# Block-summary attention and two feed-forward layers: the first batch's values loaded whole and summed from the window tiles, four groups scored without a key copy, and the start-up order written out

## The chip, the cores and the metric

One core of a Trainium2 chip runs the whole kernel. The metric is the device time of one execution in microseconds (us); of several runs the median counts. The engines are named as the profile names them: PE (TensorE), DVE (VectorE), ACT (ScalarE), POOL (GpSimd), and SP (SyncE), which here only issues DMAs.

## The reference

Attention with a local window and block summaries, then two feed-forward layers in a row. Cut to what matters:

```python
# q, k, v: (B=2, H=8, S=768, D=64); block 32, window 16; nb = 24 blocks
k_sum = k.reshape(B, H, nb, 32, D).max(axis=3)
v_sum = v.reshape(B, H, nb, 32, D).mean(axis=3)
scores_l = where(|i - j| < 16, q @ k.T / 8, -1e9)
scores_s = q @ k_sum.T / 8 + log(32)
a = softmax(concat([scores_l, scores_s]))
x = a @ concat([v, v_sum])                    # -> (1536 tokens, 512)
h = x @ w_in;  x = maximum(0.01 * h, h) @ w_out        # 512 -> 2048 -> 512
h = x @ w_in2; out = (h * tanh(softplus(h))) @ w_out2
```

All inputs are float32, and the weights are split in the kernel into a high and a low part, so that each product is three passes on PE.

## The kernel before

**Attention.** Tokens and heads are cut into 24 groups: group g is one batch, one chunk of 256 tokens and one pair of heads (four pairs for a chunk, so groups 0 to 3 are the first chunk of batch 0, 0 to 11 are batch 0). A group goes through these steps. The one-letter names are those that the change uses, and the prediction uses them for both kernels, though only the kernel after has them in its code.

- q, v: DMA of the group's queries (`load_q`, 128 KB) and of its window of values (`load_vw`, 192 KB, into rows 0 to 95 of a tile `vw`, whose rows 96 to 119 are to hold the block means).
- C, D: POOL lays the group's keys (C, two instructions) and block maxima (D) into a tile `kw` of 120 columns for each 64 queries (`k_window`, L261).
- S: PE computes the scores (L367), in 16 instructions for a group. M: DVE adds the mask and finds the maxima (L381). E: ACT takes the exponentials (L391). I: DVE inverts the sums (L400, L401). N: POOL multiplies (L406).
- T: PE transposes (L412). P: ACT or DVE copies the result out of PSUM (L420, L422). A: PE multiplies by `vw` (L431). X and L: high part (ACT L448 or DVE L450) and low part (DVE L446) of the result go into the tile x.
- K, k, J: block maxima of the keys (`k_sum`, DVE L298) for batch 0 (K) and 1 (J, with the DMAs k).
- s, p: the block means of the values of batch 0. Before, two DMAs of 768 KB bring all values of batch 0 once more (`load_v0`), PE sums them with a matrix of 1/32 (`sum_v0`, L317), and ACT or DVE copies the sums from PSUM into rows 96 to 119 of four `vw` tiles (`place_v0`, L327, L329). The four tiles serve all chunks; only their rows 0 to 95 are loaded anew for a new chunk, once A of the chunk before has read them. Batch 1 has its own way (r, R, Z: `load_vs`, `sum_vs`, `place_vs`).

**Feed-forward.** The weights come in blocks of 512 KB: w is the DMA, t (ACT L130) and m (DVE L137) build the float, h (ACT L166 or DVE L164) and l (POOL L173) split it. PE works through slots: U.2n and U.2n+1 are the two halves of slot n's product with `w_in` (L465), G and g the activation (ACT L476, L477, DVE L481), O.2n and O.2n+1 the halves of its product with `w_out` (L520), three slots later. Slots 0 to 2 take the first 256 tokens with the weight rows 0 to 2, slots 3 to 5 the next 256 tokens, slots 6 to 8 all 512 tokens with rows 3 to 5; U.12 is the first half-slot of 512 tokens.

**Order.** From the start to the end of attention (15 slots) the order of the steps is made by a planner in the kernel, `run_order` (L829): each step has a duration, an engine, needs, a due time and buffers to take, and the planner simulates the engines and writes the steps out. PE, ACT, DVE and POOL then run their instructions in exactly that order; an instruction that waits holds up all that stands behind it on its engine. The DMAs go out of SP in the order written, and at most eight are in flight (a DMA takes over the semaphore of the one eight places ahead of it and waits for its landing). In gaps that the planner sees on PE it puts `warm`, products of zeros that go nowhere. After slot 15 the rest of the kernel is written plainly, and is the same in both kernels.

Of the kernel before, what the change touches and what calls it, by code (L numbers as in the profile page):

```python
# [28 lines left out]
def kernel(  # L29
# [274 lines left out]
    def load_v0(i, eng):  # L304
        t = bigp.tile([P, 3, H * D], F32, tag=f"big{i}", name="v0")
        dma(eng, t, v0[i * 3 * P:(i + 1) * 3 * P, :].rearrange("(t p) f -> p t f", p=P))
        vraw[0, i] = t

    def sum_v0(i, tag):
        if i == 0:  # L310
            vs[0] = bank(tag)
        t = vraw.pop((0, i))

        for j in range(3):
            x = 4 * (3 * i + j)
# [109 lines left out]
    def av(g):  # L425

        px, t = st[g]
        w = vw[groups[g][2]]
        for n in range(NB):
            for s in range(2):  # L430
                nc.tensor.matmul(  # L431
                    px[s * D:(s + 1) * D, n * QB:(n + 1) * QB],
                    w[:, n, s, :],
                    t[:, s * (NB // 2) + n // 2, (n % 2) * QB:(n % 2 + 1) * QB],
                    start=True, stop=True,
                )
        st[g] = px
# [137 lines left out]
    if True:  # L575
# [48 lines left out]

        store = {
            "bank": ["a0", "a1", "y0", "y1", "y2", "y3"], "h": ["h", "h"], "raw": [0] * 3, "top": [0] * 2,
            "mid": [0] * 4, "q": [], "kw": [0] * 4, "s": [0] * 4, "pT": [0] * NPT, "g": [0] * (LAG + 1), "t": [0] * 2,
        }
        held = {}
        closed = [False]  # L630

        def load(fn, mb, needs=(), turn=0.0, take=(), give=()):
            return step({"SP": mb}, fn, needs, turn, take, give)

        def later(f, *a):
            return lambda eng: f(*a)

        def given(x, end):
            x.end = end
            return x  # L640


        landed = [4.1, 5.4, 7.7, 9.0]
        K = {(0, h): given(step({}, None), landed[h]) for h in range(4)}
        Q = {g: given(step({}, None), landed[g] + 0.2) for g in range(4)}
        W_LOAD, W_TOP, W_MERGE, W_HI, W_LO = {}, {}, {}, {}, {}

        def need_slot(i):
            return i if i < 2 * nA else 100

        for i in range(2 * nA):
            u = need_slot(i)
            W_LOAD[i] = load(later(w_load), 0.524, [], max(u - 7, -4.1) if i else -5, [("raw", ("raw", i))])
        for i in range(2 * nA, 2 * nA + 7):
            W_LOAD[i] = load(later(w_load), 0.524, [], 8 + i - 2 * nA, [("raw", ("raw", i))])
        V0 = [load(later(load_v0, i, SP), 0.786, [], -4.7 + i / 10) for i in range(2)]
        VW = {g: load(later(load_vw, g, SP), 0.196, [], -4.4) for g in range(4)}
        SUM0 = []
        for i in range(2):
            def f(eng, i=i):  # L660
                sum_v0(i, held["vs"])
            SUM0.append(step({"PE": (0.9, 0)}, f, [V0[i]] + SUM0, -4, [("bank", "vs")] if i == 0 else ()))
        PLACE = {}
        for h in range(4):
            def f(eng, h=h):
                place_v0(h, eng)
            PLACE[0, h] = step(
                {"act": (0.58, 0), "dve": (0.69, 0)}, f, [SUM0[1]], -4 + h / 10, (), ["vs"] if h == 3 else (), h
            )
# [368 lines left out]
```

## Time and profile before

| | |
|---|---|
| time, median of 3 runs | 607.79 us (606.29 to 608.97) |
| profiled execution | 608.53 us, of which its span is 606.4 us |
| PE busy | 596.3 us, 98% of the span, 3334 matmul instructions |
| DVE, ACT, POOL busy | 382.4, 314.1, 194.0 us |
| DMA | 52.10 MB, mean 86 GB/s |
| mean granted TensorE clock | 0.994 |

The profile is of one execution. PE is busy nearly all the time, so the page's table of costly groups says little about a change at the start; what is to be read there are the first 70 us, by stretches, by the order of time on PE, and by the landings of the DMAs. A granted clock of 1.00 is 2.4 GHz, 0.50 is 1.2 GHz.

### The profile page before, as it was taken

How to read it: one execution, taken by the hardware profiler on the slowest of the kernel's cores; microseconds unless marked ns; L12 is line 12 of the kernel's file. 1: busy time of each engine (PE TensorE's matmuls, PEld its weight loads, DVE VectorE, ACT ScalarE, POOL GpSimd, SP SyncE). 2: the span in 40 equal slices, each digit the busy share in tenths (PEclk: the TensorE clock that was granted, in tenths of full speed). 3: DMA queues.
4: the chain of work that ended last, by engine and by line, in shares of the span. 5: the costliest groups of instructions: out<-in, count | busy, mean ns of one | idle time of the engine just before them, and what ended most of it. 6: DMA issues, size and time to landing. Idle time of an engine off the chain costs nothing.

```text
span 606.4 us, 9153 instructions
## 1 busy us (share of the span) xinstructions
PE 596.3 (98%) x3334; PEld 485.9 (80%) x3334; DVE 382.4 (63%) x777; ACT 314.1 (52%) x671; POOL 194.0 (32%) x214
## 2 busy tenths in 40 slices
PE   9889999999989999999999999999999999999997
PEld 7789878787868888888888888888888888888885
DVE  6779777356541113112636898777699998778684
ACT  4868957447762223123665745444457555445442
POOL 6657643245430001001631233323322322332221
PEclk9979999999999999999999999999999999999999
DMA  9986554016851000002346310000021000001011
GB/s 325 358 270 211 168 191 124 2 36 217 264 178 36 0 2 0 1 0 70 123 135 234 99 35 1 0 1 0 1 70 71 0 1 1 1 34 37 0 71 69
DMA packets 19373, 52.10 MB, mean 86 GB/s; under 512 B 2176, under 2 KB 5248, under 8 KB 19072
## 3 DMA queue, kind: packets, MB, share of 16 engines
q1 hardware_dynamic: 18752, 51.00, 24.9%
q8 instruction: 26, 0.43, 0.3%
q10 hardware_dynamic: 576, 0.52, 0.3%
q14 instruction: 19, 0.16, 0.1%
HBM read 48.37 MB, written 3.15 MB: 85 GB/s over the span
## 4 chain that ended last, share of the span: by engine, by line
PE 89%; DMA 4%; ACT 3%; DVE 2%; POOL 1%; issue 1%; SPq 0%; DVEq 0%; ACTq 0%
PE h L465 40%; PE y L527 21%; PE y L520 19%; DMA raw<-in_moe_w_out_dram 3%; PE a L431 2%; PE a L367 2%; PE a L412 2%; ACT top L130 1%; DVE mid L137 1%; PE y L541 1%; PE h L220 1%; DMA kT<-in_kT_dram 1%; POOL w L173 1%; DMA raw<-in_moe_w_in_dram 1%; ACT g L477 0%
## 5 line engine op out<-in xcount | busy, mean ns | idle before, releaser
L465 PE MATMUL h<-x,w 128*128 128x512 f32 (+1 forms) x1188 | 289.7, 390 | 0.2 <-POOL w L173 0.2
L465 PEld LDWEIGHTS h<-x,w 128*128 128x128 f32 x1188 | 219.0, 189 | 49.7 <-ACT g L477 0.4
L520 PE MATMUL y<-g,w 128*128 128x512 f32 (+1 forms) x612 | 145.6, 384 | 2.1 <-ACT yp L557 1.7
L527 PE MATMUL y<-w,g 128*128 128x512 f32 x552 | 136.9, 394 | 0.0
L194 POOL TENSOR_TENSOR g<-e,g 128x512 fp32r<-128x512 f32 x47 | 73.9, 1572 | 186.9 <-ACT g L191 179.4
L520 PEld LDWEIGHTS y<-g,w 128*128 128x128 f32 x612 | 110.0, 188 | 26.8 <-ACT yp L557 2.2
L527 PEld LDWEIGHTS y<-w,g 128*128 128x128 f32 x552 | 103.8, 188 | 24.0
L173 POOL TENSOR_TENSOR w<-mid,w 128x512 fp32r<-128x512 f32 x45 | 62.9, 1405 | 122.2 <-ACT w L166 117.9
L481 DVE TENSOR_TENSOR g<-t,g 128x512 fp32r<-128x512 f32 (+1 forms) x51 | 34.5, 679 | 89.6 <-ACT g L477 89.6
L137 DVE SCALAR_TENSOR_TENSOR mid<-raw,top 128x512 int32<-128x512 int32 x64 | 55.3, 871 | 29.9 <-POOL w L173 23.7
L476 ACT ACTIVATE t<-h 128x512 f32<-128x512 f32 (+1 forms) x51 | 28.9, 567 | 83.5 <-PE h L465 83.5
L130 ACT ACTIVATE top<-raw 128x512 f16<-128x512 bf16 x64 | 50.6, 796 | 29.0 <-DMA raw<-in_moe_w_out_dram 12.6
L492 ACT ACTIVATE e<-h 128x512 f32<-128x512 f32 x48 | 28.6, 597 | 70.8 <-PE h L465 64.2
L503 DVE SCALAR_TENSOR_TENSOR u<-u,r 128x512 f32<-128x512 f32 x48 | 37.1, 773 | 25.4 <-ACT r L496 25.1
L495 ACT ACTIVATE r<-u,two 128x512 f32<-128x512 f32 x48 | 34.8, 724 | 30.7 <-DVE u L494 30.7
L391 ACT ACTIVATE s<-s,nm 128x120 f32<-128x120 f32 x96 | 36.5, 382 | 18.0 <-DVE nm L381 17.8
L166 ACT CAST w<-mid 128x512 fp32r<-128x512 f32 x62 | 37.8, 618 | 14.1 <-DVE mid L137 8.3
L191 ACT CAST g<-e 128x512 fp32r<-128x512 f32 x48 | 29.5, 615 | 18.1 <-DVE e L505 17.9
L494 DVE SCALAR_TENSOR_TENSOR u<-e 128x512 f32<-128x512 f32 x48 | 34.6, 721 | 1.1
L406 POOL TENSOR_TENSOR s<-s,r 128x480 f32<-128x480 f32 x24 | 24.7, 1033 | 31.9 <-DVE r L401 29.8
L504 DVE SCALAR_TENSOR_TENSOR u<-u,r 128x512 f32<-128x512 f32 x48 | 33.2, 691 | 1.4
L505 DVE SCALAR_TENSOR_TENSOR e<-e,u 128x512 f32<-128x512 f32 x48 | 33.1, 690 | 1.1
(71 smaller groups left out, 444.4 us busy)
## 6 DMA issues: line engine op xcount, KB each, us to landing
raw<-in_moe_w_in_dram SPq DMA_DIRECT2D x32, 512.0 KB, 4.0
raw<-in_moe_w_out_dram SPq DMA_DIRECT2D x32, 512.0 KB, 3.5
vw<-in_vW_dram SPq DMA_DIRECT2D x24, 192.0 KB, 4.3
kT<-in_kT_dram SPq DMA_DIRECT2D x8, 400.0 KB, 7.2
out_dram<-yp SPq DMA_DIRECT2D x12, 256.0 KB, 2.0
q<-in_qT_dram SPq DMA_DIRECT2D x20, 128.0 KB, 5.1
vS<-in_vS_dram SPq DMA_DIRECT2D x2, 1024.0 KB, 6.4
v<-in_v_dram SPq DMA_DIRECT2D x2, 768.0 KB, 7.8
```

Source lines behind the costliest of these rows:

```text
L130: nc.scalar.mul(out=do, in_=di, mul=4.0)
L137: nc.vector.scalar_tensor_tensor(out=d, in0=wraw.pop(i)[:, 0:2 * DM].rearrange("p (f w) -> p f w", w=2)[:, :, 1], scalar=13, in1=wtop.pop( ...
L166: nc.scalar.copy(out=w[:, 0], in_=wmid[i])
L173: (eng or nc.gpsimd).tensor_sub(out=w[:, 1], in0=wmid.pop(i), in1=w[:, 0].bitcast(F32))
L194: (nc.vector if lo == "dve" else nc.gpsimd).tensor_sub(out=dst_lo, in0=src, in1=dst_hi.bitcast(F32))
L391: nc.scalar.activation(out=s[:, n], in_=s[:, n], func=AF.Exp, scale=-1.0, bias=nm[:, n:n + 1], accum_out=sm[:, n:n + 1],)
L465: nc.tensor.matmul(ph[:, 0:n], w[:, a, kt * P:(kt + 1) * P], x[:, c, kt, o:o + n], start=(kt == 0 and i == 0), stop=(kt == KT - 1 and i == 2),
L494: V.scalar_tensor_tensor(out=u, in0=e, scalar=2.0, in1=e, op0=ALU.add, op1=ALU.mult)
L495: nc.scalar.activation(out=r, in_=u, func=AF.Ln, bias=two[:, 0:1])
L503: V.scalar_tensor_tensor(out=u, in0=u, scalar=2.0, in1=r, op0=ALU.add, op1=ALU.mult)
L520: mm = nc.tensor.matmul(y[d][:, o:o + n], w[:, a, d * P:(d + 1) * P], g[:, c, 0:n], start=sta and not second, stop=sto,)
L527: nc.tensor.matmul(y[d], g[:, a, d * P:(d + 1) * P], w[:, c], start=sta, stop=sto,)
```

## The change

- The planner goes. A string, ORDER, lists every step up to the end of attention; a suffix a, d or p names the engine where there is a choice, and the names behind a colon are the PSUM banks.
- All twelve `vw` tiles of batch 0 exist at once (groups 4 to 11 in the two tiles `big0`, `big1`), all are loaded at the outset, and `sum_v0` sums from them in three parts (s.0 to s.2). The DMAs `load_v0` go. The sums are copied into four tiles from PSUM as before (p.0 to p.3), and from these into the other eight (p.4 to p.11) by DVE or POOL.
- Groups 0 to 3 are scored straight from the loaded keys and from the maxima: no C and D, and two products where there was one (96 and 24 columns), so 32 instructions for a group.
- Groups 4 to 7 are scored and multiplied singly, not in pairs. Their queries, and the weight blocks 3 and 4, are loaded early into a tile `early`, in the place of a part of x that is needed later.
- `warm` multiplies 128x128 by 128x128, where it was 64x64 by 64x128; there are 4, 3, 2 and 1 of them in the order, behind the ten at the outset, which stay.
- Some steps change engine (t.0, t.8 and t.12 go from ACT to POOL).

```diff
+    ORDER = """
+        q.6 K.0 C.4 q.5 q.4 K.1 C.5 S.0:a0,a1 q.7 D.5 S.1:y0,y1 D.4 v.2 M.0 C.6 E.0 w.0 K.2 v.1 C.7 v.3 warm.4
+        S.2:a0,a1 I.0 v.0 K.3 N.0 v.5 v.6 M.1 D.6 v.11 warm.3 T.0:y2 E.1 D.7 v.4 M.2 S.3:y0,y1 P.0d v.7 E.2
+        S.4:a0,a1 t.0p I.1 v.8 M.3 v.10 C.8 M.4 E.3 v.9 D.8 warm.2 s.0:y0 N.1 w.1 I.2 w.2 m.0 E.4 T.1:a0 w.3 I.3 N.2
+        S.5:a1,y1 q.9 P.1d q.8 h.0a N.3 M.5 T.2:y3 w.4 E.5 s.1 P.2d l.0 w.5 I.4 k.0 T.3:a1 s.2 I.5 N.4 P.3a k.2 N.5
+        T.4:y1 p.1a p.0d p.2a p.5d p.8p p.3a p.9d warm.1 A.2 p.6d q.11 t.1a C.9 p.4d A.0 p.11d t.2a X.2d p.7p A.1
+        L.2 X.0a T.5:y0 v.12 p.10p P.4d X.1a A.3 k.1 P.5a L.1 q.10 D.9 L.0 S.6:a0,y3 X.3a L.3 U.0 C.10 M.6 k.3 E.6
+        S.7:a1,y2 D.10 m.1 A.5 M.7 C.11 w.6 h.1a A.4 I.6 D.11 X.5a S.8:a0,a1 t.3a N.6 L.5 v.14 J.0 X.4a E.7 C.12
+        T.6:y0 q.13 L.4 U.1 l.1 J.2 q.12 v.15 G.0 I.7 m.2 U.2 P.6a v.13 m.3 t.4a U.3 w.7 J.1 N.7 h.2a A.6 t.5a M.8
+        l.2 T.7:y1 X.6a G.1 P.7d h.3a D.12 U.4 M.9 C.13 E.8 A.7 D.13 L.6 l.3 J.3 S.10:a0,a1 r.0 E.9 I.8 g.0 g.1 q.14
+        U.5 M.10 N.8 q.15 X.7a U.6 L.7 G.2 C.14 I.9 U.7 E.10 M.11 C.15 O.0 N.9 U.8 E.11 I.10 D.15 U.9 D.14 N.10
+        T.8:a0 G.3 I.11 T.9:a1 m.4 P.8a O.1 P.9a R.0 N.11 U.10 h.4a t.6a m.5 A.8 R.1 l.4 t.7a w.8 U.11 h.5a R.2 X.8a
+        O.2 l.5 X.9a L.8 O.3 L.9 g.2 S.12:a0,a1 R.3 G.4 O.4 g.3 Z.0 q.16 M.12 C.16 q.17 O.5 G.5 C.17 r.1 M.13 E.12
+        O.6 D.17 D.16 O.7 g.4 g.5 m.6 T.10:a0 E.13 T.11:a1 I.12 t.8p w.9 O.8 P.10d P.11a N.12 O.9 I.13 h.6a O.10 m.7
+        Z.1 A.10 m.8 w.10 h.7a R.4 l.6 w.11 h.8a O.11 X.11a X.10a L.11 t.9a l.7 U.12 L.10 R.5 l.8 t.10a U.13 R.6
+        N.13 U.14 R.7 G.6 m.9 Z.2 U.15 g.6 w.12 t.11a h.9d S.14:a0,a1 m.10 G.7 l.9 w.13 U.16 h.10a q.19 M.14 E.14
...
+    RE = (3, 4)
+    IN = 4
+    SINGLE = 8
...
-        r = rawp.tile([P, 2 * DM + 2], I32, tag="raw", name="raw")
+        r = re[cnt["load"] - RE[0]] if cnt["load"] in RE else rawp.tile([P, 2 * DM + 2], I32, tag="raw", name="raw")
...
+            nc.gpsimd.tensor_scalar(out=do, in0=di, scalar1=4.0, scalar2=1.0, op0=ALU.mult, op1=ALU.mult)
...
     vw = [ap1.tile([WN, NB, 2, D], F32, name=f"vw{i}") for i in range(H // 2)]
+    for c in range(1, S // GT):
+        t = bigp.tile([P, H // 2, NB, 2, D], F32, tag=f"big{c - 1}", name="vw")
+        vw += [t[0:WN, i] for i in range(H // 2)]
...
-            nc.tensor.matmul(idle["p"][0:QB, 0:w], t[0:D, 0:QB], t[0:D, 0:w], start=True, stop=True)
+            nc.tensor.matmul(idle["p"][:, 0:P], t, t, start=True, stop=True)
...
+    early = xp.tile([P, 2 * KT * TB], F32, tag="x1", name="early")
+    qe = [early[:, i * GT:(i + 1) * GT].rearrange("p (t n) -> p t n", n=NB) for i in range(4)]
...
-        t = qt[g % len(qt)]
+        t = qe[g - 4] if 4 <= g < 8 else qt[g % len(qt)]
...
+        for n in range(NB):
+            x = GT // SB * c + QB // SB * n
             for hp in range(H // 2):
                 nc.tensor.matmul(
                     vs[0][32 * hp:32 * hp + NS, 0:2 * D],
-                    ind[:, NS - 4 - x:2 * NS - 4 - x], t[:, j, 2 * hp * D:2 * (hp + 1) * D],
-                    start=(i == 0 and j == 0), stop=(i == 1 and j == 2),
+                    ind[:, NS - 2 - x:2 * NS - 2 - x], vw_of(4 * c + hp)[0:WK, n].rearrange("p s d -> p (s d)"),
+                    start=(c == 0 and n == 0), stop=(c == S // GT - 1 and n == NB - 1),
                 )
...
+        if g >= H // 2:
+            i = vw_of(g % (H // 2))[WK:WN].rearrange("p n s d -> p n (s d)")
+            if eng == "dve":
+                nc.vector.tensor_copy(out=o, in_=i)
+            else:
+                pool_copy(o, i)
+            return
...
+            if g < IN:
+                w = kraw[b, hp]
+                parts = [(0, WK, lambda r, n: w[r, c * GT + n * QB:c * GT + n * QB + WK]), (WK, WN, lambda r, n: ksum[b, hp][r])]
+            else:
+                w = kwin.pop(g)
+                parts = [(0, WN, lambda r, n: w[r, n])]
...
-        batches = [[g] for g in range(4)] + [[g, g + 1] for g in range(4, NG, 2)]
+        batches = [[g] for g in range(SINGLE)] + [[g, g + 1] for g in range(SINGLE, NG, 2)]
...
-            for x in run_order():
-                if x.fn is not None:
-                    x.fn(x.eng)
+            for word in ORDER.split():
+                name, _, banks = word.partition(":")
+                eng = engines.get(name[-1])
+                name = name.rstrip("adp") if eng else name
+                if name.startswith("warm"):
+                    warm(int(name[5:]))
+                else:
+                    run[name](eng, banks.split(",") if banks else None)
```

## Rows read from the trace of the kernel before

**Rows 1.** Busy time by stretch: PE, PEld, DVE, ACT, POOL, PEclk, DMA share, GB/s

```profile
0.00:18.10 18.10, 16.77 (x166) 14.30 (x166) 11.61 (x50) 9.31 (x36) 10.78 (x39) 1.00 0.93 332
...
30.00:35.00 5.00, 3.47 (x41) 2.90 (x42) 4.32 (x16) 3.96 (x17) 4.48 (x9) 0.74 1.03 335
35.00:40.00 5.00, 5.00 (x26) 4.88 (x26) 3.93 (x7) 1.96 (x6) 1.32 (x5) 0.57 0.78 233
...
60.00:70.00 10.00, 10.00 (x136) 8.56 (x135) 8.59 (x37) 8.95 (x31) 4.44 (x6) 1.00 0.65 201
```

**Rows 2.** Order of time on PE: start us, us, line, op, names, shape, count

```profile
6.95 1.09 PE L367 MATMUL y<-kw,q 64*64 64x120 f32 x16 [0.17 <-POOL kw L257]
...
17.36 0.86 PE L317 MATMUL y<-v,ind 128*24 128x128 f32 x24
...
32.81 1.98 PE L431 MATMUL a<-pT,vw 120*64 120x64 f32 x32 [1.10 <-DVE pT L422]
...
41.91 1.46 PE L520 MATMUL y<-g,w 128*128 128x256 f32 x10 [0.31 <-POOL w L173]
...
44.01 1.23 PE L367 MATMUL a<-kw,q 64*64 64x120 f32 x32
45.17 1.70 PE L520 MATMUL y<-g,w 128*128 128x256 f32 x12
...
53.20 1.06 PE L412 MATMUL a<-ident,s 128*120 128x128 f32 x8
...
56.19 3.06 PE L465 MATMUL h<-x,w 128*128 128x512 f32 x12
...
69.61 2.96 PE L465 MATMUL h<-x,w 128*128 128x512 f32 x12
```

**Rows 3.** Order of time on SP's queue: DMA issues, start us, us, names, count

```profile
4.32 0.33 SPq L87 DMA_DIRECT2D raw<-in_moe_w_in_dram  x1
...
6.00 2.72 SPq L87 DMA_DIRECT2D vw<-in_vW_dram  x4
8.84 1.31 SPq L87 DMA_DIRECT2D raw<-in_moe_w_in_dram  x2
```

**Rows 4.** DMAs of 4.3, 6.0, 8.4, 8.84, 9.8 and 18.1 us: KB, us to landing

```profile
raw<-in_moe_w_in_dram SPq DMA_DIRECT2D x1, 512.0 KB, 5.5
...
vw<-in_vW_dram SPq DMA_DIRECT2D x1, 192.0 KB, 8.6
...
vw<-in_vW_dram SPq DMA_DIRECT2D x1, 192.0 KB, 8.2
...
raw<-in_moe_w_in_dram SPq DMA_DIRECT2D x1, 512.0 KB, 9.0
...
raw<-in_moe_w_in_dram SPq DMA_DIRECT2D x1, 512.0 KB, 10.6
...
q8 instruction: 1, 0.02, 46.2%
```

**Rows 5.** DVE by line and form, 4 to 130 us: count, busy us, mean ns

```profile
L446 DVE TENSOR_TENSOR x<-a,x 128x256 fp32r<-128x256 f32 x22 | 8.6, 419 | 1.9 <-ACT x L448 1.7
...
L298 DVE TENSOR_REDUCE ks<-kT 128x24 f32<-128x768 f32 x8 | 7.5, 939 | 1.0 <-DMA kT<-in_kT_dram 1.0
L422 DVE COPY pT<-a 120x512 f32<-120x512 f32 x11 | 7.4, 688 | 6.5 <-PE a L412 6.4
...
L164 DVE CAST w<-mid 128x512 fp32r<-128x512 f32 x2 | 0.8, 410 | 0.0
```

**Rows 6.** Order of time on DVE: start us, us, line, op, names

```profile
15.18 0.28 DVE L381 CUSTOM_DVE_ANT_0 s<-a,mask 128x120 f32<-128x120 f32 x1 [0.32 <-PE y L367]
...
15.99 0.16 DVE L400 TENSOR_SCALAR r<-sm 128x4 f32<-128x4 f32 x1
...
16.29 0.66 DVE L137 SCALAR_TENSOR_TENSOR mid<-raw,top 128x512 int32<-128x512 int32 x1
...
21.21 0.76 DVE L446 TENSOR_TENSOR x<-y,x 128x256 fp32r<-128x256 f32 x2
```

More of the change, by code (lines that the diff above doesn't have):

```diff
@@ L80 @@
     ident = const.tile([P, P], F32, name="ident")
-    ind = const.tile([P, 2 * NS - 4], F32, name="ind")
+    ind = const.tile([WK, 2 * NS - 2], F32, name="ind")
     two = const.tile([P, 1], F32, name="two")
@@ L208, with vw_of, warm @@
     vw = [ap1.tile([WN, NB, 2, D], F32, name=f"vw{i}") for i in range(H // 2)]
+    for c in range(1, S // GT):
+        t = bigp.tile([P, H // 2, NB, 2, D], F32, tag=f"big{c - 1}", name="vw")
+        vw += [t[0:WN, i] for i in range(H // 2)]
+    def vw_of(g):
+        return vw[g if g < len(vw) else g % (H // 2)]
     idle = {}
-    def warm(n, w=128):
+    def warm(n):
         if not idle:
-            idle["t"] = ap1.tile([P, 128], F32, name="idle")
+            idle["t"] = ap1.tile([P, P], F32, name="idle")
             nc.vector.memset(idle["t"], 0.0)
@@ L302, with sum_v0 @@
     vs = {}
[L304 to L315, printed above, removed]
+    def sum_v0(c, tags=None):
+        if c == 0:
+            vs[0] = bank(tags[0])
+        for n in range(NB):
+            x = GT // SB * c + QB // SB * n
             for hp in range(H // 2):
@@ L423, in p_evac, with av @@
         st[g] = (pp, t)
[L425 to L437, printed above, removed]
+    def av(gs):
+        for g in gs:
+            px, t = st[g]
+            w = vw_of(g)
+            for n in range(NB):
+                for s in range(2):
+                    nc.tensor.matmul(
+                        px[s * D:(s + 1) * D, n * QB:(n + 1) * QB],
+                        w[:, n, s, :],
+                        t[:, s * (NB // 2) + n // 2, (n % 2) * QB:(n % 2 + 1) * QB],
+                        start=True, stop=True,
+                    )
+            st[g] = px
     def x_part(g, c, eng):
@@ L625 @@
[L625 to L640, printed above, removed]
@@ L643 @@
[L643 to L655, printed above, removed]
@@ L656, with step @@
-        V0 = [load(later(load_v0, i, SP), 0.786, [], -4.7 + i / 10) for i in range(2)]
-        VW = {g: load(later(load_vw, g, SP), 0.196, [], -4.4) for g in range(4)}
-        SUM0 = []
+        run = {}
+        def step(name, fn, *a):
+            run[name] = lambda eng, banks: fn(*a, *([eng] if eng else []), *([banks] if banks else []))
+        for i in range(2 * nA + 7):
+            step(f"w.{i}", w_load)
+        for i in range(2 * nA + 4):
+            step(f"t.{i}", w_scale)
+            step(f"m.{i}", w_merge, False)
+            step(f"h.{i}", w_hi)
+            step(f"l.{i}", w_lo)
@@ L659 @@
         for i in range(2):
[L660 to L663, printed above, removed]
+            step(f"r.{i}", load_vs, i, SP)
+            for q in range(4):
+                step(f"R.{4 * i + q}", sum_vs, i, q)
         for h in range(4):
[L665 to L669, printed above, removed]
@@ new lines, with up_half, act, down_half @@
+        for gs in batches:
+            step(f"S.{gs[0]}", scores, gs)
+            step(f"A.{gs[0]}", av, gs)
+        def up_half(n, half):
+            _, _, _, j, o, N, _, sidx, _ = slots[n]
+            if half == 0:
+                gq[n] = up_begin(n)
+            up(sidx, j, o, N, gq[n], half)
+        def act(n, second):
+            N = slots[n][5]
+            gq[n] = leaky_b(*gq[n], N) if second else leaky_a(gq[n], N)
+        def down_half(m, half):
+            nonlocal cur_y
+            _, layer, _, _, o, N, i, sidx, last = slots[m]
+            if i == 0 and o == 0 and half == 0:
+                cur_y = new_y()
+            down(sidx, layer, i == 0, last, o, N, gq[m], cur_y, half)
+            if half == 1:
+                gq.pop(m)
@@ new lines, in drain_half @@
+        def drain_half(j, eng):
+            drain(0, 0, j, 0, TB, cur_y, eng)
+        for n in range(X):
+            step(f"G.{n}", act, n, 0)
+            step(f"g.{n}", act, n, 1)
+            for half in range(2):
+                step(f"U.{2 * n + half}", up_half, n, half)
+                step(f"O.{2 * n + half}", down_half, n, half)
+        for j in range(2):
+            step(f"d.{2 * j}", drain_half, j, "act")
+            step(f"d.{2 * j + 1}", drain_half, j, "dve")
+        engines = {"a": "act", "d": "dve", "p": "pool"}
```

338 lines of the change are left out of this document (62 added, 276 removed).

## The prediction

> **What bounds the kernel now.** I read the stretches first. From 60 to 70 us PE is busy all 10.00 us at granted clock 1.00; from 30 to 35 us it is busy 3.47 of 5 us, and the clock falls to a mean of 0.74, then 0.57 [rows 1]. Then PE in order of time: its last idle stretch is 0.31 us before 41.91, where O.1 waits for POOL's l.3 [rows 2]. From there PE is the bound without a gap, and only work that stands ahead of 41.91 can be gained or lost. So I need one point behind which both orders have the same PE work. U.16 is that point: in both lists the scores, transposes, products with values and half-slots ahead of it are the same set. Before, U.16 starts at 69.61 [rows 2]. **The forecast is the new start of U.16**; the rest shifts with it.
>
> **Part 1, the value sum.** Out go two loads of 768 KB; eight window tiles of 192 KB come forward. The DMAs are the bound of this part: their share from 0 to 18 us is 0.93 [rows 1]. Tiles issued at 6.00 and 8.41 (the first and fourth of the group, which ends at 8.72) land after 8.6 and 8.2 us, at 14.6 and 16.6: 0.66 us a tile [rows 3, 4]. The first weight block lands at 4.32 + 5.5 = 9.8 [rows 3, 4]. In the new order four loads of queries and all twelve tiles are added to what had landed by then. 128 KB is priced between 0.3 us (a weight block's 1.2 us for 512 KB, 16.6 to 17.8, by bytes) and 0.44 (a tile's 0.66 by bytes); I take 0.36. So the last tile (v.9) lands at 9.8 + 4 x 0.36 + 12 x 0.66 = 19.2.
>
> One thing is added. The weight block issued at 8.84 lands at 17.8, the next, issued at 9.80 (0.35 us before its group ends), at 20.4: 2.6 us where 1.2 is usual, and at 18.1 a 16 KB instruction packet goes through [rows 3, 4]. I read the excess as that packet holding up one of the 16 engines on which every load waits. By 18.1 PE had run 166 matmuls with as many weight loads [rows 1]. The new order has 20 warm, 4 x 32 scores, 16 more, 4 transposes and 18 warm before s.0: 186. So the packet falls at about 12 us, ahead of the values, and I add 1.2: v.9 at 20.4. The other end is no addition; that is a rival. In a sentence of its own: the Trainium skill, page "Runtime: NRT & Kernel Launch", section "Instruction fetch mechanics", says that instructions are streamed in blocks of 16 KiB and that crossing a block's boundary is mostly hidden; the row speaks against "hidden" where the queue of loads is full, and by the rule v.9 would land at 19.2.
>
> s.2 is 32 instructions of a kind of which 24 took 0.86 us with the tail of the last [rows 2], so 0.8 to 1.1; 0.8 up to the point where the next step starts. It ends at 21.3; before, the sum was over at 18.2. **So the sum comes later, not earlier.** That is paid for by what is done meanwhile: by 21.3 groups 0 to 5 are scored, of 0 to 3 all transposed and of 4 the transposition follows.
>
> **Part 2, from the sum to U.7.** In the new list DVE stands without a hole between s.2 and L.7, on which U.7 waits. Its steps, each at its duration less 0.07 (the next starts before the last has ended: two L of 0.42 take 0.76 together [rows 5, 6]):
> - p.0 from PSUM 0.62 (as P, 0.69 [rows 5]); five copies p.5, p.9, p.6, p.4, p.11. A copy of 24x512 inside SBUF is not in the trace; the nearest forms are L164 with 512 elements and both sides in SBUF, 0.41, and the copies out of PSUM, 0.69 [rows 5]. I take the first: 5 x 0.35 = 1.75; the other end adds 1.4.
> - X.2 0.46; eight L 2.8 [rows 5]; two P 1.24; two g 0.7 (like L).
> - five M: from 15.18 to the next step at 15.99, 0.81 each [rows 6], 4.1. Three I: 15.99 to 16.29, 0.3 each, 0.95. Three m: 0.66 less overlap, 1.8 [rows 6].
> - four J: 0.87 each, 3.5 [rows 5].
>
> The sum is 17.9 us; waits on ACT's X and on S.6 add 0.5 by the list. From 21.5 (s.2 plus 0.2 to the first copy) L.7 ends at 39.9. POOL and ACT run beside it: the chains l.1 to l.3 hold U.2 and U.4 for under 1 us each, ahead of U.7, so they are inside that wait.
>
> **Part 3, from U.7 to U.16.** Here PE has everything. U.7 is 0.77 (O.2 and O.3, two halves of 256 tokens from 45.17, take 1.70 with the tail of the last, 1.55 without it [rows 2]) and ends at 40.7. Sixteen such halves (O.0 to O.11, U.8 to U.11) 12.3; four half-slots of 512 tokens 5.9 (twelve instructions in 2.96 [rows 2] with their tail); S.12 and S.14 1.16 each, 2.3 (44.01 to 45.17); T and A of groups 8 to 11: between 53.20 and 56.19 stand a T pair, one half and an A pair, so 2.2 a time, 3.7 by the better of the two places (the others start without a switch). Together 24.2: **U.16 at 64.9**.
>
> I also went through both written lists step by step with these durations. The order of before comes out at 69.1, 0.5 early against the trace's 69.61; I put that on the new one: 65.4, **4.2 us earlier**.
>
> **What costs nothing, and its cover.** The 64 more score instructions of groups 0 to 3 and the bigger warm run before 12.6, when PE waits for values until 15.3 anyway. t.0 moves to POOL and waits there for w.0 (13.4); N.1, N.2, N.3 and with them T.1 stand behind it. N.1 ends at 16.3, T.1 at 16.7, and behind T.1 on PE s.1 waits for v.7 until 18.5: covered by 1.8 us; a conversion on POOL anywhere from 0.67 (two L257 copies) to 2 us changes nothing. POOL's p.7, p.8, p.10 serve A.8, far later. Four q and blocks 3, 4 in `early` block x only until S.7 and m.4. Dropping 1.57 MB behind 20 us is nothing once PE is the bound. C and D of groups 0 to 3 go from a POOL that was busy 10.78 of 18.1 us [rows 1]: nothing.
>
> **The rivals.**
> (a) *No instruction packet in the way*: v.9 at 19.2, all behind it 1.2 earlier: gain 5.4.
> (b) *A spell at the lower clock.* Before, PE runs the first scores at half speed (16 instructions in 1.09 us at 6.95; 32 in 1.23 at 44.01) and falls to 0.5 again after a stretch with waits like the 1.10 us before 32.81 [rows 1, 2]. The new order leaves PE idle from 12.6 to 15.3, waiting for s.0, longer than that wait. If the clock falls around 16, T.1, S.5, T.2, s.1, T.3, s.2 (3.4 us of work) need 6.8, s.2 ends at 22.9 and U.16 comes 1.8 later: gain 2.4. This agrees with the Trainium skill, page "TensorE: Matmul & The Clock Gate", Part 1, "What's actually happening": the throttled clock is the default and activity releases it.
> (c) *The lower clock stays until 35 us* (slower). The steps from s.0 to U.3 are 15 us of PE work in a stretch of 19; at half speed they need 30. With part of it caught up later, U.16 comes 8.8 later: 4.6 slower than before. It decides from where the low spell lasts past about 29 us. Against it: PE is dense from 16 to 22 at half speed, and before, the clock came back at 39 under such density [rows 1].
> (d) *The change doesn't do what it says*: the tiles come later than 0.66 apart. At 1.0 us each the gain is gone.
>
> **How the numbers follow.** My sum is against the profiled execution, 608.53 us (span 606.4 and 2.1 around it): 604.3. That execution lies 0.7 above the median of the runs, 607.79, so for a median I say 607.8 - 4.2 = 603.6. Chances: forecast 0.40; (a) 0.18, 602.4; (b) 0.27, 605.4; (c) 0.07, 612.3; (d) or a copy at 0.69 eating half of it, 0.08, 605 to 608. For 8 in 10: from (a) less 1 us of spread between runs (606.29 to 608.97 before), 601.4, to no gain but the same spread, 608.0. A measurement here tells about 0.5%, 3.0 us, from no change. Faster than 604.8: the forecast and (a) whole, a little lost to the spread and a little won from (b): 0.59. Within: 0.32. Slower than 610.8: (c) and unseen stalls, 0.09.
>
> **What would show it.** Right: PE's last idle before some 42 us lies ahead of U.7 or O.0, not at 41.91; DVE is over 95% busy from 21.5 to 39.5; U.16 starts near 65.4; v.9 lands near 20.4; s.2 ends near 21.3. Step by step: landings 0.66 apart test part 1; the copies p on DVE near 0.41 test part 2; a PEclk of 1.00 from 16 to 40 us rules out (b) and (c). Wrong: an idle PE behind 45 us (then DVE or ACT is the bound for longer than I say), or a U.16 that moved while the end did not.

## The result, and the profile after

| | before | after |
|---|---|---|
| time, median | 607.3 us (606.3 to 609.0) | 612.3 us (611.4 to 616.2) |
| ratio | | 1.0112, 95% interval 1.0087 to 1.0137 |
| span of the profiled execution | 606.4 us | 610.8 us |
| PE busy | 596.3 us | 594.8 us |
| start of U.16 | 69.61 us | 70.45 us |

The forecast was 603.6 us, 4.2 us faster; by the ratio the kernel is 6.8 us slower (1.0112 of 607.3). The medians, of four runs each, are only 5.0 us apart; a second set of runs below (e3_after) gives 1.0115 and 7.1 us, so I go by the ratio. PE is busy 1.5 us less in a span that is 4.4 us longer: it waits 5.9 us more. The stretches of the kernel after, with the columns of [rows 1]:

```profile
0.00:18.10 18.10, 13.95 (x214) 12.90 (x218) 11.60 (x57) 9.58 (x42) 10.69 (x40) 0.97 0.92 274
15.00:20.00 5.00, 3.09 (x44) 2.38 (x48) 2.04 (x4) 2.24 (x11) 4.54 (x7) 0.71 1.07 283
20.00:25.00 5.00, 4.69 (x94) 3.49 (x86) 3.67 (x15) 2.78 (x10) 3.40 (x4) 0.95 1.03 335
30.00:35.00 5.00, 4.70 (x103) 4.08 (x104) 4.75 (x25) 3.75 (x15) 2.96 (x8) 1.00 1.04 322
35.00:40.00 5.00, 4.38 (x44) 3.77 (x44) 4.93 (x10) 4.47 (x14) 4.04 (x5) 1.00 1.00 269
60.00:70.00 10.00, 10.00 (x100) 8.43 (x103) 9.75 (x14) 8.21 (x19) 6.39 (x6) 1.00 0.64 214
180.00:190.00 10.00, 6.42 (x21) 4.86 (x21) 3.26 (x6) 5.57 (x10) 1.29 (x1) 0.83 0.36 127
```

Three things differ from [rows 1]. PE's products are at full pace early (eight score products of 96 columns take 0.61 us at 5.68 and 0.46 at 6.77), but between 15 and 20 us the granted clock is at 0.71 on average. From 30 to 40 us DVE is busy 9.68 of 10 us, which the forecast wanted. And there is a hole where nothing was changed: from 180 to 190 us PE is busy 6.42 us. PE in order of time, kernel after (columns as in [rows 2]):

```profile
16.91 1.78 PE L360 MATMUL y<-vw,ind 96*24 96x128 f32 x32 [2.87 <-DMA vw<-in_vW_dram]
...
22.81 1.07 PE L360 MATMUL y<-vw,ind 96*24 96x128 f32 x32
...
25.90 1.15 PE L488 MATMUL y<-pT,vw 120*64 120x64 f32 x32 [1.21 <-ACT vw L379]
...
30.08 0.38 PE L424 MATMUL a<-kw,early 64*64 64x120 f32 x2 [1.36 <-DVE x L503]
...
46.13 0.51 PE L522 MATMUL h<-x,w 128*128 128x256 f32 x2 [0.64 <-DVE x L503]
...
70.45 1.90 PE L522 MATMUL h<-x,w 128*128 128x512 f32 x7
...
180.73 0.73 PE L577 MATMUL y<-g,w 128*128 128x512 f32 x2 [0.71 <-DVE yp L616]
184.33 4.15 PE L577 MATMUL y<-g,w 128*128 128x512 f32 x10 [2.87 <-ACT yp L614]
```

Read it by points: s.0 (16.91), s.2 (22.81), A.2 (25.90), S.6 (30.08), the last of U.7 (46.13), U.16 (70.45). U.16 was forecast at 65.4: 5.05 us late, though only 0.84 later than in the trace of before. Up to the last half-slot ahead of 176 us nothing is added (175.29 before, 175.92 after). Then PE waits 3.58 us (0.71 and 2.87) where the kernel before waited 1.74 for the same thing, the copies `yp` that empty the y banks of the first part; I call them the drain. PE in the kernel before:

```profile
175.29 4.10 PE L465 MATMUL h<-x,w 128*128 128x512 f32 x17
...
181.13 3.02 PE L520 MATMUL y<-g,w 128*128 128x512 f32 x12 [1.74 <-ACT yp L557]
```

So there are two questions: why the start is late, and what happens at 180 us.

### The profile page after: what moved, and what is told of

It is laid out like the page before. It is cut to its first block, busy times and chain, and to the rows that moved or that the text cites. A ratio compares the mean times of both kernels' runs of the same rounds, so it can differ in the third digit from the quotient of the medians.

```text
span 610.8 us, 9304 instructions
## 1 busy us (share of the span) xinstructions
PE 594.8 (97%) x3440; PEld 484.7 (79%) x3440; DVE 386.8 (63%) x774; ACT 314.3 (51%) x676; POOL 196.9 (32%) x209
## 4 chain that ended last, share of the span: by engine, by line
PE 85%; DMA 6%; DVE 5%; ACT 2%; issue 1%; POOL 0%; SPq 0%; ACTq 0%; DVEq 0%
PE h L522 39%; PE y L584 21%; PE y L577 19%; DMA raw<-in_moe_w_out_dram 3%; DVE mid L169 2%; PE a L424 2%; PE a L488 1%; PE a L469 1%; DMA raw<-in_moe_w_in_dram 1%; DMA kT<-in_kT_dram 1%; DMA vw<-in_vW_dram 1%; ACT top L160 1%; PE y L598 1%; PE y L360 1%; DVE s L438 0%
## 5 line engine op out<-in xcount | busy, mean ns | idle before, releaser
L538 DVE TENSOR_TENSOR g<-t,g 128x512 fp32r<-128x512 f32 (+1 forms) x51 | 36.7, 724 | 95.2 <-ACT g L534 95.2
L169 DVE SCALAR_TENSOR_TENSOR mid<-raw,top 128x512 int32<-128x512 int32 x62 | 54.5, 890 | 32.5 <-POOL w L205 18.6
L160 ACT ACTIVATE top<-raw 128x512 f16<-128x512 bf16 x59 | 46.7, 796 | 38.4 <-DMA raw<-in_moe_w_out_dram 16.0
L448 ACT ACTIVATE s<-s,nm 128x120 f32<-128x120 f32 x96 | 36.5, 383 | 18.1 <-DVE nm L438 18.1
L554 DVE TENSOR_TENSOR e<-u,h 128x512 f32<-128x512 f32 x48 | 32.8, 684 | 1.1
```

The source lines that it names most:

```text
L169: nc.vector.scalar_tensor_tensor(out=d, in0=wraw.pop(i)[:, 0:2 * DM].rearrange("p (f w) -> p f w", w=2)[:, :, 1], scalar=13, in1=wtop.pop( ...
L448: nc.scalar.activation(out=s[:, n], in_=s[:, n], func=AF.Exp, scale=-1.0, bias=nm[:, n:n + 1], accum_out=sm[:, n:n + 1],)
L538: nc.vector.tensor_sub(out=g[:, 1, 0:n], in0=t[:, 0:n], in1=g[:, 0, 0:n].bitcast(F32))
```

## The experiments

Each kernel was timed beside the kernel before on one chip, and its ratio is against those runs.

**The part behind slot 15.** That part is written the same in both kernels, but its engine order is not written: the framework's scheduler makes it from its own estimate of the times, and what stands ahead enters that estimate. Laid side by side, the orders differ in 39 places on ACT, 18 on DVE, 146 on PE, 2 on POOL, all ahead of some 195 us. ACT in the kernel after, then in the kernel before:

```profile
181.48 0.78 ACT L160 ACTIVATE top<-raw 128x512 f16<-128x512 bf16 x1 [3.60 <-DMA raw<-in_moe_w_out_dram]
183.06 0.78 ACT L160 ACTIVATE top<-raw 128x512 f16<-128x512 bf16 x1
183.70 1.07 ACT L614 ACTIVATE yp<-y 128x512 f32<-128x512 f32 x2
```

```profile
178.25 0.80 ACT L130 ACTIVATE top<-raw 128x512 f16<-128x512 bf16 x1 [3.99 <-DMA raw<-in_moe_w_out_dram]
179.85 0.79 ACT L130 ACTIVATE top<-raw 128x512 f16<-128x512 bf16 x1
180.48 1.08 ACT L557 ACTIVATE yp<-y 128x512 f32<-128x512 f32 x2
```

In both the drain stands behind a weight conversion that waits for its block; in the kernel after the block is issued at 178.23 and not at 173.85. I fixed the order by an edge from each instruction to the one wanted ahead of it (the lists are left out):

```diff
+        for e, text in PIN.items():
...
+            for a, b in zip(want, want[1:]):
+                tc.add_manual_dep(at[e][b], at[e][a].name, ...)
```

The changed kernel in the order of before:

> The changed kernel, with the plainly written part behind slot 15 put into the engine order that it has in the kernel before (the instructions are the same; the framework had put 39 places on ACT, 18 on DVE, 146 on PE and 2 on POOL otherwise). Theory O: the changed kernel's loss behind U.16 is that order; ACT's drain of the y banks stands behind a weight conversion whose block lands 3 us later, PE waits 3.6 us instead of 1.74 and runs 3.4 us at half clock. Then PE's wait at the drain is 1.7 us again, the clock does not fall at 184 us, and the time is that of the kernel before plus the 0.8 us by which U.16 is late: 608 us, ratio 1.001. Rival S: the order of the first 135 us leaves the weight pipeline in another state (blocks that land later), and the stall comes whatever the order behind it: 612 us, ratio 1.008 or more.

Measured: 610.9 us, ratio 1.0062 (1.0038 to 1.0086). PE waits 2.09 us at the drain and the clock does not fall there; U.16 starts at 71.77, and one new wait (0.70 us for ACT's g at 96.57) comes in. So 0.5% is gained against 1.0112, as theory O wants, but 3.8 us stay where 0.8 were expected.

The kernel before in the order of after:

> The kernel before, with the plainly written part in the engine order that it has in the changed kernel. Theory O: the stall moves here: PE waits 3.6 us at the drain near 180 us, the clock falls there, 610.5 to 611 us, ratio 1.006. Rival S: the kernel before keeps its 1.7 us wait and its time, 607.3 us.

Measured: 608.7 us, 1.0038 (1.0019 to 1.0058), less than the 610.5 to 611 expected. Its PE at the drain:

```profile
177.55 0.73 PE L520 MATMUL y<-g,w 128*128 128x512 f32 x2 [0.41 <-DVE yp L559]
181.21 4.14 PE L520 MATMUL y<-g,w 128*128 128x512 f32 x10 [2.93 <-ACT yp L557]
```

The stall has moved with the order, and with it the fall of the clock (0.50 from 181.4 to 184.8). Theory O holds and rival S falls: the order is worth 0.5% in the changed kernel and 0.4% in the kernel before. Next, the drain is put ahead, in both kernels (on DVE its two copies go ahead of one step). On ACT:

```diff
-L130 ACTIVATE top<-raw
-L476, L477 (activation)
-L130 ACTIVATE top<-raw
 L557 ACTIVATE yp<-y  (two)
+L476, L477 (activation)
+L130 ACTIVATE top<-raw
+L130 ACTIVATE top<-raw
```

> The kernel before, with the four drain copies of the last block of the first part (two on ACT, two on DVE) and one activation put ahead of the weight conversion on which ACT waits 3.99 us; nothing else is moved. If the drain's place on ACT is what PE waits for, the 1.74 us wait at 181 us goes and the time is 605.5 us, ratio 0.997. If the activation or the weights behind it are late next, PE waits later and the time stays at 607.3.

Measured: 604.7 us against 606.4, 0.9973 (0.9961 to 0.9985); from 175 to 195 us PE is busy all 20 us (18.26 in the kernel before, 16.42 after).

> The changed kernel with the same order as in the run before this one (the order of the kernel before, the drain put ahead). Theory O: 606.3 us, 0.8 above the kernel before with the drain put ahead; that difference is then the whole effect of the written order of the first 70 us. Rival S: still a wait of PE at 180 us, and 609 us or more.

Measured: 608.2 us, 1.0032 (1.0017 to 1.0046), no wait of PE at 180 us. Against the kernel before with the same drain (0.9973) the written start alone costs 0.59%, 3.6 us. The trace had said 0.84. The reason is in the other traces of the start of before: U.16 is at 67.64 (order_a) and 66.39 (drain), not at 69.61. The execution that I read had the clock at 0.50 from 32.4 to 39.3 us [rows 1]; these two did not. The kernel itself does not always pay that spell, and I had counted it. The times say the same: that execution's mean granted clock is 0.994, and of the 109 runs of the kernel before that were timed beside the experiments only 6 have 0.994 or less, while 50 have 0.999 or 1.000.

**The start**, with e1_after_drain as the base, whose part behind slot 15 has no stall that would cover a gain. All edits are in ORDER. The kernels of this part are within 0.4% of each other but for e2_copies_pool, and most of their intervals overlap the base's (1.0017 to 1.0046): what each edit does is read from its trace.

```diff
-v.9 D.8 warm.2 s.0:y0
+v.9 D.8 warm.14 s.0:y0
```

> The changed kernel with the drain put ahead (e1_after_drain), and 14 warm products ahead of s.0 where there are 2, so that PE is busy while it waits for the values (idle 2.3 to 3.2 us before s.0 in three traces, the clock at 0.5 from 17 us for 3.4 to 6.8 us in all three). Theory: that wait brings the clock down; filled, PEclk stays 1.00 from 16 to 25 us and s.0 takes 1.07 instead of 1.8. How much it gives: if the values are late anyway (s.2 waits for v.9), U.16 moves by 0.3 us or less; rival: the spell costs what rival (b) of the prediction said, 1.8 us.

Measured: the granted clock stays at 1.00 until PE's work ends, and s.0 takes 1.07 us. U.16 is at 69.31 where the base has 69.72, so the rival's 1.8 us are not there; 607.7 us, 1.0012 (0.9992 to 1.0032). In all twelve runs of this kernel the mean granted clock is 0.999 or 1.000, and it is still 0.4% behind the kernel before with its drain ahead (0.9973): the clock alone does not make the 3.6 us.

```diff
-q.6 K.0 C.4 q.5 q.4 K.1 C.5 S.0:a0,a1 q.7 D.5 S.1:y0,y1 D.4 v.2 M.0 C.6 E.0 w.0 K.2
+w.0 q.6 K.0 C.4 q.5 q.4 K.1 C.5 S.0:a0,a1 q.7 D.5 S.1:y0,y1 D.4 v.2 M.0 C.6 E.0 K.2
```

> e1_after_drain with the load of the first weight block as the first DMA of SP's list behind the keys, ahead of the four early queries, instead of between the first and the second window tile. Theory: that block among the tiles costs more than its bytes (v.2 lands at 10.6 and v.1 at 14.4 to 15.1, where block and tile are worth 1.9 us); then v.9 lands near 20.4 instead of 21.7 to 22.9, s.2 and U.16 come 1.5 us earlier, 606.6 us. Rival: the loads are bound by bytes and by the instruction packet; v.9 lands at 22 as before, and the time stays at 608.

Measured: v.9 lands at 21.06, U.16 at 69.19; 606.9 us, 1.0003 (0.9984 to 1.0023). Inconclusive: the nine traces with w.0 in its old place have v.9 anywhere from 20.88 to 22.97, and e3_combined, with w.0 in front, at 22.17.

```diff
-p.5d p.8p p.3a p.9d warm.1 A.2 p.6d q.11 t.1a C.9 p.4d A.0 p.11d t.2a X.2d p.7p
+p.5d p.3a p.9d warm.1 A.2 p.6d q.11 t.1a p.4d A.0 p.11d t.2a X.2d C.9 p.7p
...
-v.12 p.10p P.4d
+v.12 p.8p P.4d
...
-E.8 A.7 D.13
+E.8 A.7 p.10p D.13
```

> e1_after_drain with POOL's copies p.8, p.7, p.10 and the key step C.9 put behind DVE's five copies p.5, p.9, p.6, p.4, p.11, beside which they ran. Theory: a DVE instruction with both sides in SBUF waits for the instruction that POOL is in; alone, a 24x512 copy takes 0.41 us or less and the five take 2.0 us instead of 2.9, so U.7 comes 1 us earlier. Rival: 0.64 us is what this copy costs on 24 partitions, and neither the copies nor U.7 move.

Measured, DVE by line and form from 4 to 60 us (columns as in [rows 5]), first e1_after_drain, then this kernel:

```profile
L371 DVE COPY vw<-vw 24x512 f32<-24x512 f32 x5 | 2.9, 644 | 0.0
```

```profile
L371 DVE COPY vw<-vw 24x512 f32<-24x512 f32 x5 | 1.8, 417 | 0.0
```

The same copy takes 0.64 us on average beside POOL's work and 0.42 without, so it is not long by itself. A.2 to U.16 takes 43.72 us instead of 44.56; 607.2 us, 1.0009 (0.9986 to 1.0031).

```diff
-p.5d p.8p p.3a p.9d warm.1 A.2 p.6d q.11 t.1a C.9 p.4d A.0 p.11d t.2a X.2d p.7p
+p.5p p.4p p.3a warm.1 A.2 q.11 t.1a C.9 A.0 t.2a X.2d p.6p p.7p
...
-v.12 p.10p P.4d
+v.12 P.4d
...
-N.6 L.5 v.14
+N.6 L.5 p.9p p.8p v.14
...
-E.8 A.7 D.13
+E.8 A.7 p.10p p.11p D.13
```

> e1_after_drain with the five copies p.5, p.9, p.6, p.4, p.11 on POOL instead of DVE (POOL makes all eight, the last four later). If DVE's own list is the bound from s.2 to U.7, as predicted, 2.9 us go from it and U.7 comes 2 to 2.9 us earlier: 605.5 us. Rival: DVE is slowed by POOL's work, and more work on POOL slows it more; DVE's steps I and m stretch, and U.7 gains less than 1 us: 607.5 us or more.

Measured: 610.8 us, 1.0062 (1.0037 to 1.0087). S.6 comes earlier (3.19 us behind A.2 instead of 4.18), then U.1 waits 2.64 us for POOL's l: the rival was right, and by more than it said.

**The bank, and the pieces together.**

```diff
-p.1a p.0d p.2a p.5d
+p.1a p.2a p.0a p.5d
```

> e1_after_drain with the copy p.0 on ACT instead of DVE (order p.1, p.2, p.0, p.3, all on ACT). In five traces ACT's p.1, DVE's p.0 and ACT's p.2 stand one behind the other though they are on two engines and write three tiles; they read one PSUM bank. Theory: the bank is what orders them, and p.0 on DVE holds up p.2 and with it A.2 by its 0.7 us. Then A.2 comes 1.65 us behind the start of the last instruction of s.2 instead of 2.34 in all five, and U.16 46.2 us behind it instead of 46.9; 607.4 us. Rival: A.2 waits for P.2 or for the values, and the distance stays at 2.34.

Measured: A.2 1.57 us behind the start of s.2's last instruction (2.29 in the base by the same reading), U.16 45.7 instead of 46.9. ACT in the base, DVE in the base, ACT in this kernel:

```profile
23.21 0.57 ACT L379 COPY vw<-y 24x512 f32<-24x512 f32 x1 [0.45 <-PE y L360]
24.53 1.18 ACT L379 COPY vw<-y 24x512 f32<-24x512 f32 x2 [0.75 <-DVE vw L377]
```

```profile
23.82 0.68 DVE L377 COPY vw<-y 24x512 f32<-24x512 f32 x1 [1.86 <-ACT vw L379]
```

```profile
24.58 2.38 ACT L379 COPY vw<-y 24x512 f32<-24x512 f32 x4 [0.45 <-PE y L360]
```

In the base the two engines take turns: ACT waits for DVE's copy and DVE for ACT's, though they read different rows of the bank and write different tiles. With all four copies on one engine these waits are gone. Time: 607.0 us, 1.0004 (0.9987 to 1.0022).

The next kernel has the edits of e2_weights_first, e2_pool_later and e3_sums_act, and `warm.10` ahead of s.0:

> All that helped in one kernel: e1_after_drain with the first weight block loaded first, 10 warm products ahead of s.0, POOL's copies behind DVE's, p.0 on ACT. If the pieces add, U.16 comes 45.3 us behind the last instruction of s.2 (46.9 less 0.7 less 0.85), v.9 lands near 21, U.16 starts near 67.5 and the time is 605.5 us, ratio 0.999; that is still no better than the kernel before with the drain put ahead (0.997), whose U.16 started at 66.4. If they do not add, U.16 stays behind 69 and the time above 607.

Measured: 605.2 us, 0.9975 (0.9962 to 0.9989). v.9 at 22.17, A.2 1.56 behind the last of s.2, but U.16 45.9 behind it, not 45.3: the two gains on DVE do not add. It is faster than the kernel before, and no better than that kernel with its drain ahead (0.9973).

In e1_before_drain:

```diff
-            nc.tensor.matmul(idle["p"][0:QB, 0:w], t[0:D, 0:QB], t[0:D, 0:w], start=True, stop=True)
+            nc.tensor.matmul(idle["p"][:, 0:P], t, t, start=True, stop=True)
```

> e1_before_drain with the bigger warm products alone (128x128 by 128x128, as the changed kernel has them; nothing else of the change). In the traces of the kernel before the clock rises at 14.6 to 17.5 us, in those of the changed kernel at 4.6 to 7.1. Theory: the size of the warm products makes that difference; the clock is 1.00 from about 7 us here too, and the first scores run in half the time. As PE waits for keys and POOL then, it gives less than 0.5 us: 604.5 us. Rival: the earlier clock is due to the denser scores of groups 0 to 3; then the clock rises at 15 us still.

Measured: 603.4 us, 0.9946 (0.9929 to 0.9964), the fastest of all. The clock is at 1.00 from 6.4 us, so the size of the warm products made that difference. U.16 is at 66.13 although the fourth key block lands 1.0 us later than in e1_before_drain.

And the changed kernel as it is:

> The changed kernel itself once more, beside the others: is the stall at the drain there in every execution, or was it one execution's? By theory O PE waits again 3.6 us near 180 us and the clock falls behind it, U.16 starts between 69.3 and 71.8 as in the other five orders of this start, and the time is 1.0 to 1.1% above the kernel before: 612.5 us. If it was chance, the wait at 180 us is under 2 us and the time is 609.

Measured: 614.1 us, 1.0115 (1.0090 to 1.0139); PE waits 0.85 and 2.98 us at the drain, the clock is at 0.50 from 187.4 to 190.8, U.16 at 71.99. The stall was not one execution's chance.

**Two points that were left.** In `score_norm`:

```diff
         s, r = st[g]
+        if g in (7, 8):
+            return
```

> e1_after_drain without POOL's products N.7 and N.8 (the scores of groups 7 and 8 stay undivided by their sums; this part of the computation is left out). From S.6 to U.7 the six traces of this order take 16.05 us where 14.17 were predicted, and three DVE steps there last until the end of what POOL is in: an I at 0.55 instead of 0.16 (beside l.1), m.3 at 1.48 instead of 0.69 (beside N.7), two g at 1.52 instead of 0.75 (beside N.8). Theory: DVE is the bound there and those steps wait for POOL; without N.7 and N.8, m.3 and the two g are 0.8 us shorter each and S.6 to U.7 takes 14.4 to 14.7 us. Rival: DVE's steps are long by themselves, or another engine is the bound there: 15.8 us or more.

Measured: DVE in the base, POOL in the base, DVE in this kernel:

```profile
35.46 0.55 DVE L457 TENSOR_SCALAR r<-sm 128x4 f32<-128x4 f32 x1
...
36.72 1.48 DVE L169 SCALAR_TENSOR_TENSOR mid<-early,top 128x512 int32<-128x512 int32 x1
...
42.67 1.52 DVE L538 TENSOR_TENSOR g<-t,g 128x256 fp32r<-128x256 f32 x2
```

```profile
34.70 1.28 POOL L205 TENSOR_TENSOR w<-mid,w 128x512 fp32r<-128x512 f32 x1
36.37 1.28 POOL L463 TENSOR_TENSOR s<-s,r 128x480 f32<-128x480 f32 x1 [0.38 <-DVE r L458]
```

```profile
39.32 0.69 DVE L169 SCALAR_TENSOR_TENSOR mid<-early,top 128x512 int32<-128x512 int32 x1
...
44.63 0.90 DVE L540 TENSOR_TENSOR g<-t,g 128x256 fp32r<-128x256 f32 x2
```

POOL's l ends at 35.98, and the I that began beside it at 36.01; N.7 ends at 37.65, and m.3 ends 0.55 behind that. Without N.7, m.3 is back at 0.69; the two g take 0.90 and not 1.52. S.6 to the end of L.7 takes 14.7 us instead of 16.0, S.6 to U.16 39.1 instead of 40.4. DVE was the bound, and POOL made its steps long. (This kernel leaves work out, so its time is not compared.)

The bigger warm alone (the edit of e3_before_warm, in the kernel before with its own order fixed):

> The kernel before with the bigger warm products alone, and its own order behind slot 15. In three traces of its start with the small ones the clock rose at 14.6 to 17.5 us, and in one of the three it fell again from 32.4 to 39.3; with the big ones it rose at 6.4. Theory: an early clock keeps those later falls away in most executions, and the kernel gains the 1.3 us by which e3_before_warm (0.9946) is ahead of e1_before_drain (0.9973): ratio 0.997, 605.3 us. Rival: the start gives nothing, since PE waits for data there anyway, and the two ratios differ by chance: 1.000.

Measured: 605.6 us, 0.9986 (0.9971 to 1.0002). U.16 at 64.95, no spell in the first 70 us, but PE's 1.77 us wait at the drain is followed by 0.50 from 177.0 to 180.4. By the times alone it can't be told from no change, and the interval of e3_before_warm touches that of e1_before_drain; what the bigger warm is worth in time is open. For the start there are two pairs of traces, in the second table below.

The starts of the changed kernel side by side, from the traces (us; "low" is a stretch at granted clock 0.50 ahead of 45 us):

| | v.9 lands | A.2 | S.6 | U.16 | low | ratio |
|---|---|---|---|---|---|---|
| after | 22.47 | 25.90 | 30.08 | 70.45 | 17.1-20.5 | 1.0112 |
| e3_after | 22.49 | 27.41 | 31.60 | 71.99 | 16.7-23.5 | 1.0115 |
| e1_after_order_b | 22.97 | 27.22 | 31.40 | 71.77 | 16.6-23.4 | 1.0062 |
| e1_after_drain | 21.71 | 25.16 | 29.34 | 69.72 | 17.2-20.6 | 1.0032 |
| e2_warm | 21.62 | 24.74 | 28.92 | 69.31 | none | 1.0012 |
| e2_weights_first | 21.06 | 24.62 | 28.80 | 69.19 | 16.3-19.7 | 1.0003 |
| e2_pool_later | 22.69 | 26.48 | 29.66 | 70.20 | 14.9-21.7 | 1.0009 |
| e2_copies_pool | 20.88 | 24.74 | 27.93 | 70.82 | 17.4-20.9, 37.9-41.3 | 1.0062 |
| e3_sums_act | 22.48 | 25.80 | 29.58 | 69.96 | 15.6-22.4 | 1.0004 |
| e3_combined | 22.17 | 24.57 | 28.34 | 68.89 | none | 0.9975 |
| e4_no_norm | 22.38 | 27.77 | 31.95 | 71.06 | 17.1-24.0 | - |

From A.2 on the first six are the same to 0.03 us (44.55 to 44.58 to U.16): what varies from execution to execution lies ahead of A.2, in the landings and the clock.

The starts of the kernel before ("rise" is where the record of the granted clock begins, with 1.00):

| | fourth key block lands | rise | U.16 | low |
|---|---|---|---|---|
| before | 8.39 | 15.4 | 69.61 | 32.4-39.3 |
| e1_before_drain | 8.36 | 14.6 | 66.39 | none |
| e4_before_warm_only | 8.43 | 6.3 | 64.95 | none |
| e1_before_order_a | 9.32 | 17.5 | 67.64 | none |
| e3_before_warm | 9.40 | 6.4 | 66.13 | none |

At like landings, with one trace of each, the spell makes U.16 3.2 us later (69.61 against 66.39), and the bigger warm makes it 1.4 and 1.5 us earlier.

## Why the prediction was wrong, point by point

- **"The rest shifts with it": wrong, 3.2 us.** 1.0115 less 1.0062 is the order behind slot 15 (2.3 us the other way round, in the kernel before). I had taken "written plainly, and the same" for "executed in the same order". "From there PE is the bound without a gap" was not so even before: the wait of 1.74 us at 181.13 was in the trace, and I did not ask what made it.
- **The baseline: 2 to 3.2 us too late.** U.16 at 69.61 contains a spell at half clock (PEclk 0.74 and 0.57 [rows 1]) that four other traces with the start of before, two with the bigger warm among them, do not have (64.95 to 67.64). I read those rows, and used the spell against the new order as rival (b) without asking whether the old one pays it each time. Only 0.7 us was taken off for it.
- **Part 1, landings: v.9 at 22.47, forecast 20.4.** The 16 KB packet came at 10.6 us, ahead of the values as said, and took 0.95. From the second tile (v.1) to the last the tiles were 0.71 apart on average, not 0.66; the four tiles of the kernel before are 0.69 apart too (14.59 to 16.65), and the landings of [rows 4], rounded to 0.1 us, had hidden it. That makes 0.5 us. The other 1.6 were there by v.1, which landed at 15.37 where the sum has 13.8. What they are stays open: moving w.0 did not settle it, and one start varies by 2 us.
- **Rival (b), the clock: it happened.** In all nine traces with PE idle 2.0 to 3.7 us ahead of s.0 the clock falls, at 14.9 to 17.4 us; in the two kernels that fill this wait with warm products (1.2 us of it stay in e3_combined) it never does. The mechanism was right; the chance of 0.27 was too low for what came in all nine. For the price I read the way from v.9 to the last instruction of s.2: 0.84 us without a spell, 1.1 to 1.6 with one of 3.4 us, 1.5 to 3.1 with one of 6.8. So the 1.8 us of the prediction are too much for the short spell, which the changed kernel's first trace has, and inside the range of the long one. PE idle, then 0.50, and 1.00 again under work at 20.5 us: this agrees with the Trainium skill, "TensorE: Matmul & The Clock Gate", "What's actually happening", cited for it there.
- **Rival (c), 612.3 us: the measured median by luck.** It stood for a low clock until 35 us. In the two traces of the changed kernel the clock is back at 20.5 and 23.5.
- **Part 2, the sum of DVE's list: 18.6 us forecast from the end of s.2 to the end of L.7 (21.3 to 39.9), 22.2 measured (23.9 to 46.1).** Terms of the sum were mis-sized, 3.6 us in all. The first copy p.0 began 0.7 us behind s.2, not 0.2, because it waited for ACT's copy from the same bank (without that taking of turns A.2 comes 0.7 earlier, e3_sums_act). The five copies took 2.91, not 1.75; 0.41 was right for a copy alone (e2_pool_later). m.3 was 0.8 longer and the two g together another 0.8 (e4_no_norm: 1.3 of both), an I 0.4. The bound was the one named, DVE; that POOL beside it makes its steps longer was put at nothing, without a reason. The row was there: the kernel before has an m of 1.77 us beside POOL's l (131.77). The Trainium skill, "SBUF — State Buffer", "SBUF: two separate sides", says that POOL's instruction and a DVE instruction that needs the port pair they share exclude each other for the whole instruction; this is the rule that spoke against the change, and I did not bring it. The trace agrees: m.3 takes 1.48 us beside N.7 and 0.69 without it. For the bank, the Trainium skill, "PSUM — Partial Sum Buffer", "PSUM bank collisions raise a hardware error", has software guard PSUM by bank and 32-partition quadrant, and calls guarding by bank the simple version. The four sums lie in four such quadrants of one bank, so by that rule the copies could have run side by side; no run tried it.
- **Part 3 was right within 0.4 us.** From U.7's end (46.64) to U.16 it took 23.8 us, forecast 24.2; PE has no wait there.
- **"DVE over 95% busy", "PE's last idle ahead of U.7": right from 25 us on** (9.68 of 10 us from 30 to 40), wrong from 21.5 to 25 (3.67 of 5 us from 20 to 25). And the last sentence of the prediction (a U.16 that moves while the end does not) described the second half of the loss, without a chance being given to it.

Taken together: U.16 5.05 us late, the baseline some 2.7 too late and the order 3.2 turn 4.2 us gained into 6.8 lost. The 2.7 is what the times leave (3.6 less 0.84), so that sum closes by its making; the traces give 2 to 3.2 for it.

## What to carry to other kernels

When a scheduler orders what comes behind an edit, compare the order of the unchanged part before any time is forecast: here half of the loss was there, and fixing the order both showed it and, with the drain put ahead, won 0.3% on the kernel before. Sum an engine's list with what runs beside it: here a DVE copy with both sides in SBUF took 0.42 us alone and up to 0.84 beside POOL, and two engines that emptied one PSUM bank took turns. Ask whether a spell at low clock in the execution that you read belongs to the kernel, and put work into a wait of PE that brings one on.

## What the runs showed of the hardware

- With warm products of 64x64 by 64x128 the clock rises at 14.6 to 17.5 us (three traces of the start of before); with products of 128x128 by 128x128, and nothing else changed in the start, at 6.3 and 6.4. These are the times at which the trace's record of the granted clock begins, with 1.00. Ahead of them there is no record and the PEclk column reads 1.00 all the same, so the slow pace is seen in the products alone: in the kernel before four transposes take 1.11 us at 13.01 and 0.65 at 15.98.
- Waits of PE of 2.87 to 2.98 us at the drain were followed by 3.4 us at half clock in all three traces that have them; waits of 1.74 to 2.09 us in one of three. The wait of 2.64 us for POOL's l in e2_copies_pool was followed by 3.4 us too (37.9 to 41.3).
- In the kernel after, the first instruction of a step I (128x4, both sides in SBUF) takes 0.15 to 0.17 us in the twelve cases where POOL is idle as it starts. In the other twelve it starts while POOL is in an instruction, and it always lasts past the end of that instruction, up to 0.94 us (17.98, beside an N).
- The window tiles land slower than other loads. The kernel before, 9 to 14 us (both loads of 768 KB), then the kernel after, 12 to 20 us (the last column is GB/s):

```profile
9.00:14.00 5.00, 5.00 (x36) 4.41 (x34) 3.22 (x14) 2.61 (x12) 3.62 (x9) 1.00 1.05 376
```

```profile
12.00:20.00 8.00, 5.13 (x96) 4.12 (x95) 4.81 (x25) 5.24 (x27) 4.79 (x7) 0.82 1.05 269
```

Fetching the values once, in tiles of 96 rows, moves fewer bytes at a lower rate. Whether the 96 rows are the reason, no run here separates.
